# First expert's weights and early rows: a generator that runs beside the attention is started eight steps sooner and spread out

## The chip, the cores and the metric

One core of one Trainium2 chip. The metric is the device time of one launch in microseconds (us): 1130.11 us is the median of three runs before the change (1129.94 to 1133.36).

## What is computed

A decaying-attention layer on 8 x 8 heads of 576 positions, then two mixture-of-experts layers on the 4608 resulting rows of 512 numbers. In the first, each row goes to the expert with the largest logit; in the second, experts take rows greedily, 576 each.

```python
ret = scores * Dmat[None, :, :, :]              # scores = q k^T / 8, Dmat[i, j] = gamma^(i-j) for i >= j
x = np.matmul(ret, v)                           # to rows of 512: 4608 x 512
expert_idx = np.argmax(x @ w_gate, axis=1)      # first layer
for e in range(8):
    xe = x[expert_idx == e]
    out[expert_idx == e] = gate_w * (np.maximum(xe @ w1[e], 0) @ w2[e])
# second layer: the same two matmuls, with rows assigned in order of their logits, at most 576 to an expert
```

## The kernel before

**Attention** (`attention`) handles 36 tiles of 128 rows (t = 0 to 35), software-pipelined: one step `s` of the loop at its end calls each stage for another tile (loads six ahead, q and k transposed two ahead, scores one ahead, logits two behind). For a tile, PE makes the scores (24 small matmuls, L184) in the PSUM tile `pS`; DVE masks them into `sh` (L187); PE subtracts what was rounded off (L189) and DVE makes the remainder `sl` (L191); PE multiplies by the values and the running state (L214, `pO`), DVE scales the rows into `xr` (L245), PE transposes them (L152), ACT splits them (L158, L160) and PE makes eight logits (L262). There is one `pS`: the next tile's scores wait until `sl` of this one is written. Transposes, logits and the lists below share three PSUM tiles `tp`. Every three or four tiles `route` chooses experts on DVE (L273 to L288), and SP then stores the rows to `Xs`.

**Beside it runs the generator `early`**, resumed once a step from step `AFTER` on. It (1) loads the four parts of expert 0's first weight and splits each into two fp16 halves (`load_half`: ACT casts, L384; DVE or GpSimd subtracts), (2) counts which of the first 27 tiles' rows go to expert 0 and makes a list of 384 of them (matmuls L668, L669, L560; DVE rows `nA`, `G`, `lw`, `ix`, L670 to L675, L537 to L569), (3) gathers these rows with three indirect DMAs from GpSimd (L418), into the memory that later holds the second weight, and (4) normalises each group of 128: ACT squares and sums (L430), DVE makes a power of two (L311 to L313, `scA`), ACT scales (L443), DVE subtracts (L446), SP turns the result by DMA (L457). The first expert's first layer starts on these 384 columns as soon as the attention is done; its other 256 rows are gathered after that.

**What sets the order.** The kernel is written in program order, but the tile framework reorders: it runs its own time estimate (`schedule_with_timeline_sim=True`) and writes for each engine one in-order queue. Only instructions that go through `pe(...)` or `keep_in_program_order` keep their order. An instruction whose semaphore is not there yet stops its whole queue.

**After it** `moe1` runs 8 experts (`layer1` L499, `layer2` L525) and `moe2` another 8; PE is nearly always busy there.

Of the kernel before, what the change touches and what calls it, by code (L numbers as in the profile page):

```python
# [21 lines left out]
BIG = 1048576.0  # L22
TA = 27
SA = 3
AFTER = 24
T0 = (76, 88)
LATE = 3
SOON = 3
# [72 lines left out]
def attention(k, q, kk_, v, wg1, X, after):  # L101
# [197 lines left out]
    for s in range(-7, NT + 5):  # L299
        store(2 if s < NT + 2 else 36)  # L300
        for f, off in stages:
            if 0 <= s - off < NT:
                f(D[s - off])
        if s >= AFTER:
            next(after, None)
# [108 lines left out]
def gather(k, src, gidx, M=128, xg=None):  # L414
    nc = k.nc
    if xg is None:
        xg = k.fp.tile([128, W], F32, name="xg", bufs=6)
    nc.gpsimd.indirect_dma_start(out=xg[:M], out_offset=None, in_=src,  # L418
                                 in_offset=bass.IndirectOffsetOnAxis(ap=gidx[:M], axis=0))
    return xg  # L420
# [15 lines left out]
def normalise(k, xg, dve=False, to=None, pin=False):  # L436


    nc = k.nc
    h, sc = to or (k.fp.tile([128, 1024], F16, name="xhl", bufs=2), k.fp.tile([128, 6], F32, name="sc", bufs=12))  # L440
    x = xg[:, :512]
    scale2(k, x, sc, h[:, 0:512], dve, pin)
    d = nc.scalar.activation(h[:, 0:512], x, AF.Copy, scale=sc[:, 1:2])  # L443
    if pin:
        pe(k, d)
    nc.vector.scalar_tensor_tensor(h[:, 512:1024], x, sc[:, 1:2], h[:, 0:512], op0=OP.mult, op1=OP.subtract)  # L446
    nc.vector.tensor_scalar(sc[:, 3:4], sc[:, 2:3], 2.0 ** -14, None, op0=OP.mult)
    nc.gpsimd.tensor_copy(sc[:, 4:6], xg[:, 512:514])
    return h, sc


def turn(k, x, xT, s, M=128, dma=True):

    nc = k.nc
    S = slice(s * 128, s * 128 + M)
    if dma:
        nc.sync.dma_start(xT[:, :, S], x[:M], transpose=True)  # L457
        return
    pt = k.fps.tile([128, 8, 128], F16, name="tp")
    for c in range(8):  # L460
        pe(k, nc.tensor.transpose(pt[:, c, :M], x[:M, c * 128:(c + 1) * 128], k.idh[:M, :M]))
    nc.scalar.activation(xT[:, 0:4, S], pt[:, 0:4, :M], AF.Copy)
    nc.vector.tensor_copy(xT[:, 4:8, S], pt[:, 4:8, :M])


def new_xT(k):
    k.xn += 1
    return (k.xp if k.xn % 2 else k.fp).tile([128, 8, CAP1], F16, name="xT", bufs=1)
# [74 lines left out]
def lists(k, V, nt, base, end, n, slot, twice=False, begun=None, more=None):  # L543

    nc = k.nc
    G, nV = begun or cover(k, V, nt, base, end, n * 128)
    parts = [(G[:, 0], V), (G[:, 1], nV)]  # L550
    if more:
        parts += [(more[1][:, 0], more[0]), (more[1][:, 1], more[2])]
    pl = k.tp([128, 5, NS + 4])[:, :, :nt + 4]
    for s in range(n):
        cut = [(0, 128, 128 * s)]
        if twice and s == n - 1:
            cut = [(0, 64, 128 * s), (64, 128, 128 * s)]
        for lo, hi, o in cut:
            for i, (x, y) in enumerate(parts):
                pe(k, nc.tensor.matmul(pl[lo:hi, s, :], x[:, o:o + hi - lo], y, start=i == 0, stop=i == len(parts) - 1))  # L560
    N = slice(0, n)
    w = k.lp.tile([128, 5, 6], F32, name="lw")
    nc.vector.tensor_tensor(w[:, N, 0], slot[:, N], pl[:, N, nt], op=OP.subtract)
    cm = k.lp.tile([128, 5, NS], F32, name="lc")[:, :, :nt]
    nc.vector.tensor_tensor(cm[:, N], pl[:, N, 0:nt], w[:, N, 0:1].to_broadcast([128, n, nt]), op=OP.is_le)
    nc.vector.tensor_reduce(w[:, N, 1], cm[:, N], op=OP.add, axis=AX.X)
    nc.vector.scalar_tensor_tensor(w[:, N, 2], w[:, N, 1], 128.0, pl[:, N, nt + 1], op0=OP.mult, op1=OP.add)
    ix = k.lp.tile([128, 5], I32, name="ix", bufs=3)
    nc.vector.tensor_scalar(ix[:, N], w[:, N, 2], float(128 * nt - 1), None, op0=OP.min)  # L569
    return ix, pl  # L570
# [53 lines left out]
def tables(k, V, nt, incl, base):  # L624

    nc = k.nc
    nc.vector.tensor_copy(V[:, :, 0:nt], incl)
    nc.vector.tensor_copy(V[:, :, nt], base)
    nc.vector.tensor_copy(V[:, :, nt + 1], k.c('p').to_broadcast([128, V.shape[1]]))
    nc.vector.memset(V[:, :, nt + 2:nt + 4], 1.0)  # L630
# [21 lines left out]
def early(k, X, w1):  # L652


    nc = k.nc
    first = load_half(k, k.w[0], w1, 1, 2)
    next(first)
    yield
    yield
    for _ in range(4):  # L660
        next(first, None)
        yield
    k.nA = k.cp.tile([128, 4], F32, name="nA")
    OA = k.OH[:, 0, 0:TA]
    inc = k.lp.tile([128, TA], F16, name="incA", bufs=1)
    nc.vector.tensor_tensor_scan(inc, k.one_h[:, 0:TA], OA, 0.0, op0=OP.mult, op1=OP.add)
    pb = k.tp([128, 2])
    nc.tensor.matmul(pb[:, 0:1], k.lt_h, inc[:, TA - 1:TA], start=True, stop=True)  # L668
    nc.tensor.matmul(pb[:, 1:2], k.one_h, inc[:, TA - 1:TA], start=True, stop=True)  # L669
    nc.vector.tensor_copy(k.nA[:, 0:2], pb)  # L670
    nc.vector.tensor_tensor(k.nA[:, 2:3], k.nA[:, 0:1], inc[:, TA - 1:TA], op=OP.add)
    nc.vector.tensor_scalar(k.nA[:, 3:4], k.nA[:, 0:1], -1.0, 128.0 * SA, op0=OP.mult, op1=OP.add)
    V = k.lp.tile([128, 1, TA + 4], F16, name="VA", bufs=1)
    tables(k, V, TA, inc[:, None, :], k.nA[:, 0:1])
    nc.vector.scalar_tensor_tensor(OA, inc, k.nA[:, 3:4], OA, op0=OP.is_gt, op1=OP.mult)  # L675
    ix, _ = lists(k, V[:, 0, :], TA, k.nA[:, 0:1], k.nA[:, 2:3], SA, k.slot)

    g = k.wp.tile([128, 8, 512], F16, name="w2h").rearrange("p f d -> p (f d)").bitcast(F32)
    h = k.wp.tile([128, 8, 512], F16, name="w2l").rearrange("p f d -> p (f d)")
    sc = k.cp.tile([128, SA, 6], F32, name="scA")  # L680
    rows = [gather(k, X[0:128 * TA, :], ix[:, s:s + 1], xg=g[:, W * s:W * (s + 1)]) for s in range(SA)]
    k.early = new_xT(k), []
    yield
    for s in range(SA):
        yield
        x, c = normalise(k, rows[s], to=(h[:, 1024 * s:1024 * (s + 1)], sc[:, s, :]))
        turn(k, x, k.early[0], s)
        k.early[1].append(c)
# [898 lines left out]
def program(tc, q, kk, v, wg1, w11, w12, wg2, w21, w22, consts, out, dbg=None):  # L1587
    nc = tc.nc
    ctx = ExitStack()
    k = K()  # L1590
    k.pin = False
    setup(k, tc, nc, ctx, consts)
    moe_setup(k, ctx)
    X = tc.dram_tile([128 * NT, W], F32, name="Xs")
    X1 = tc.dram_tile([128 * NS, W], F32, name="X1s")
    LG = tc.dram_tile([128 * NS, 8], F32, name="LGsd")
    g1 = split_gate(k, wg1, "wg1")
    k.wgl = split_gate(k, wg2, "wg2")
    select_setup(k)
    k.w = {0: K()}  # L1600
    attention(k, q, kk, v, g1, X, early(k, X, w11[0]))
    open_ffn(k)
    rest = moe1(k, X, X1, w11, w12)
    k.pin = False
    overflow(k, X, X1, LG, w11, w12)
    k.wn, k.xn, k.yn = 8, 9, 0
    k.pin = True
    moe2(k, X1, w21, w22, out, rest)
    k.pin = False
    anew(k, X1, w21, w22, out)  # L1610
    if dbg:
        dbg(k, X, X1, LG)
    k.fctx.close()
    ctx.close()
# [25 lines left out]
```

## Time and profile before

| | |
|---|---|
| runs | 1129.94, 1130.11, 1133.36 us |
| the profiled execution | 1129.93 us, of which the span from first to last instruction is 1128.1 us |
| PE, DVE, ACT, POOL busy | 94%, 59%, 43%, 30% of the span |
| attention | about the first 221 us |
| mean granted TensorE clock | 0.978 of full |

In a row of the timeline come the start (us), the duration, engine, line and operation, output<-inputs, shapes, and in brackets how long the engine had stood idle before and what released it. A queue is in order, so a row that waits holds all behind it.

### The profile page before, as it was taken

What the parts mean: (1) busy time and instruction counts of PE and PEld (TensorE: products, weight loads), DVE (VectorE), ACT (ScalarE), POOL (GpSimd) and SP (SyncE); (2) the same over time, 40 slices, a digit from 0 to 9 for tenths busy, and PEclk for the clock granted to TensorE, in tenths of its full rate; (3) what the DMA queues carried; (4) which work ended last, traced back from release to release, by engine and by line L of the source; (5) the groups of instructions that cost most, each with busy time, mean ns of one, the idle gap of its engine ahead of it and who ended that gap; (6) DMA issues with size and microseconds to landing.
All of it is one profiled execution on the core that took longest, in us unless ns stands there. A gap on an engine that the chain in (4) does not pass through costs nothing. (4 is left out here: it accounts for less than half of the span.)

```text
span 1128.1 us, 25795 instructions
## 1 busy us (share of the span) xinstructions
PE 1061.4 (94%) x10279; PEld 682.9 (61%) x10279; DVE 668.7 (59%) x1662; ACT 481.4 (43%) x851; POOL 340.7 (30%) x589
## 2 busy tenths in 40 slices
PE   7999999789998999999989989899999999999996
PEld 5778877555646464746457534656565656567573
DVE  5787888775648455647553476747566646634140
ACT  5777766455545354536442124322233222224231
POOL 5766775041202020212040023323324141431101
PEclk9999999799999999999989999899999999999998
DMA  9999882349767677777966025538367392784211
GB/s 239 225 252 233 204 219 74 114 160 220 179 171 169 142 192 171 178 178 196 253 143 104 11 94 149 161 102 189 110 184 182 104 214 91 175 205 142 88 62 44
DMA packets 307520, 178.32 MB, mean 158 GB/s; under 512 B 241408, under 2 KB 274176, under 8 KB 307392
## 3 DMA queue, kind: packets, MB, share of 16 engines
q1 hardware_dynamic: 296928, 144.24, 52.6%
q0 software_dynamic: 10464, 32.34, 9.3%
q8 instruction: 84, 1.38, 0.5%
q14 instruction: 44, 0.36, 0.1%
HBM read 116.82 MB, written 31.28 MB: 131 GB/s over the span
## 5 line engine op out<-in xcount | busy, mean ns | idle before, releaser
L499 PE MATMUL ph<-xT,w1h 128*128 128x320 f16 (+4 forms) x2048 | 374.3, 299 | 11.9 <-DVE sc L312 4.9
L499 PEld LDWEIGHTS <-w1h 128*128 128x128 f16 x2048 | 200.3, 100 | 89.9 <-issue 24.3
L499 PE MATMUL ph<-xT,w1l 128*128 128x320 f16 (+4 forms) x1024 | 233.8, 299 | 0.0
L525 PE MATMUL py<-w2h,hh 128*128 128x512 f16 x536 | 203.2, 379 | 2.8 <-DVE key L1268 2.2
L525 PE MATMUL py<-w2l,hh 128*128 128x512 f16 x536 | 203.3, 379 | 0.0
L525 PE MATMUL py<-w2h,hl 128*128 128x512 f16 x536 | 203.2, 379 | 0.0
L525 PEld LDWEIGHTS <-hh 128*128 128x128 f16 x1072 | 103.1, 98 | 120.1 <-issue 4.9
L504 ACT ACTIVATE hh<-ph 128x576 f16<-128x576 f32 (+4 forms) x136 | 83.3, 613 | 181.7 <-PE ph L499 177.4
L505 DVE SCALAR_TENSOR_TENSOR hl<-ph,hh 128x576 f16<-128x576 f32 (+4 forms) x136 | 97.8, 719 | 69.0 <-ACT hh L504 67.9
L499 PEld LDWEIGHTS <-w1l 128*128 128x128 f16 x1024 | 100.9, 100 | 35.6 <-issue 3.3
L387 DVE SCALAR_TENSOR_TENSOR w1l<-stage,w1h 128x1024 f16<-128x1024 f32 x62 | 75.6, 1222 | 59.2 <-ACT w1h L384 58.1
L525 PEld LDWEIGHTS <-hl 128*128 128x128 f16 x536 | 52.4, 98 | 60.3
L387 DVE SCALAR_TENSOR_TENSOR w2l<-stage,w2h 128x1024 f16<-128x1024 f32 x64 | 78.3, 1224 | 12.0 <-ACT w2h L384 10.9
L384 ACT ACTIVATE w2h<-stage 128x1024 f16<-128x1024 f32 x64 | 66.9, 1048 | 8.7 <-DMA stage<-in_moe_w_dram 8.5
L430 ACT ACTIVATE x1r<-py 128x512 bf16<-128x512 f32 x40 | 23.8, 596 | 108.9 <-PE py L525 64.9
L384 ACT ACTIVATE w1h<-stage 128x1024 f16<-128x1024 f32 x62 | 64.2, 1046 | 8.7 <-DMA stage<-in_moe_w_dram 8.7
L1446 POOL DMA_INDIRECT out_dram<-x1r,ti x20 | 21.0, 1051 | 127.5 <-ACT x1r L1445 105.7
L1446 POOL DMA_INDIRECT out_dram<-w2T,ti x20 | 22.4, 1122 | 122.7 <-ACT w2T L1445 104.4
L418 POOL DMA_INDIRECT xg<-X1s,ix x40 | 44.7, 1116 | 44.2 <-DVE zf L1372 24.3
L583 POOL COPY x1r<-sc 128x1 f32<-128x1 f32 x37 | 8.5, 232 | 158.8 <-DMA X1s<-x1r 93.0
L187 DVE TENSOR_TENSOR sh<-pS,ct 128x1024 f16<-128x1024 f32 x36 | 43.9, 1220 | 17.3 <-PE pS L184 17.2
L147 POOL TENSOR_TENSOR vl<-vf,vh 128x512 f16<-128x512 f32 x36 | 41.7, 1159 | 36.1 <-ACT vh L146 28.9
(370 smaller groups left out, 1780.1 us busy)
## 6 DMA issues: line engine op xcount, KB each, us to landing
stage<-in_moe_w_dram SPq DMA_DIRECT2D x128, 512.0 KB, 4.1
Xs<-xr SPq DMA_DIRECT2D x36, 257.0 KB, 4.4
X1s<-x1r SPq DMA_DIRECT2D x33, 257.0 KB, 3.2
k<-in_k_dram SPq DMA_DIRECT2D x32, 256.0 KB, 4.3
q<-in_q_dram SPq DMA_DIRECT2D x32, 256.0 KB, 4.1
v<-in_v_dram SPq DMA_DIRECT2D x32, 256.0 KB, 4.4
k<-in_k_dram SPq DMA_DIRECT2D x8, 128.0 KB, 3.5
q<-in_q_dram SPq DMA_DIRECT2D x8, 128.0 KB, 3.7
```

What stands on the lines that cost most here:

```text
L147: nc.gpsimd.tensor_tensor(d.vl, d.vf, d.vh, op=OP.subtract)
L187: nc.vector.tensor_tensor(f(d.sh), f(pS), both, op=OP.mult)
L384: d = nc.scalar.activation(at(h, i), t, AF.Copy, scale=128.0)
L387: d = nc.vector.scalar_tensor_tensor(at(l, i), t, 128.0, at(h, i), op0=OP.mult, op1=OP.subtract)
L418: nc.gpsimd.indirect_dma_start(out=xg[:M], out_offset=None, in_=src, in_offset=bass.IndirectOffsetOnAxis(ap=gidx[:M], axis=0))
L430: d = nc.scalar.activation(q.bitcast(mybir.dt.bfloat16), x, AF.Square, accum_out=sc[:, 0:1])
L499: pe(k, nc.tensor.matmul(ph[:, z, :b], x[:, c, F], xT[:, y + c, a:a + b], start=i == 0, stop=i == 11))
L504: nc.scalar.activation(oh, src, AF.Relu)
L505: nc.vector.scalar_tensor_tensor(ol, src, 0.0, oh, op0=OP.max, op1=OP.subtract)
L525: pe(k, nc.tensor.matmul(py, x[:, f, S], y[:, f, :], start=i == 0, stop=i == 23))
L583: nc.gpsimd.tensor_copy(xr[:, 513:514], sc[:, 5:6])
L1446: nc.gpsimd.indirect_dma_start(out=out2 if tail else out, out_offset=bass.IndirectOffsetOnAxis(ap=ti, axis=0), in_=y, in_offset=None)
```

## The change

`AFTER` goes from 24 to 16. In `early` each of the four casts of the weight now comes after three resumptions (it was one), and one resumption more lies between the gathers and the first square. Counted in resumptions, the weight parts, which fell on steps 26, 27, 28 and 29, now fall on steps 19, 22, 25 and 28; the list and the gathers go from step 30 to 31, the three groups of rows from steps 32 to 34 to steps 34 to 36.

```diff
-AFTER = 24
+AFTER = 16
...
     first = load_half(k, k.w[0], w1, 1, 2)
     next(first)
-    yield
-    yield
     for _ in range(4):
+        yield
+        yield
+        yield
         next(first, None)
-        yield
+    yield
+    yield
+    yield
     k.nA = k.cp.tile([128, 4], F32, name="nA")
...
     k.early = new_xT(k), []
+    yield
     yield
     for s in range(SA):
         yield
```

What the queues show: on SP, and for all loads and casts of the first weight on ACT, DVE and GpSimd, the order is the same before and now. What moves is the list, the gathers and the normalising of the early rows. Lines from 658 on are numbered 3 to 4 higher in the changed file.

**DVE, tiles 32 to 34.** Before, ten rows from the mask of tile 32 (the first L187; `ix` of the list stands nine rows ahead of it):

```order
L187 TENSOR_TENSOR sh<-pS,ct 128x1024
L286 TENSOR_SCALAR es<-es 128x3
L245 TENSOR_TENSOR xr<-pO,ct 128x2x4x64
L288 RECIPROCAL gt<-es 128x3
L311 TENSOR_SCALAR scA<-scA 128x1
L312 TENSOR_SCALAR scA<-scA 128x1
L313 TENSOR_SCALAR scA<-scA 128x1
L191 TENSOR_TENSOR sl<-pS,ct 128x1024
L447 TENSOR_SCALAR scA<-scA 128x1
L311 TENSOR_SCALAR scA<-scA 128x1
```

Now, from the remainder of tile 32 (the first L191) on:

```order
L191 TENSOR_TENSOR sl<-pS,ct 128x1024
L566 TENSOR_REDUCE lw<-lc 128x3
L172 SCALAR_TENSOR_TENSOR kT<-tp,kT 128x512
L567 SCALAR_TENSOR_TENSOR lw<-lw,tp 128x3
L569 TENSOR_SCALAR ix<-lw 128x3
L187 TENSOR_TENSOR sh<-pS,ct 128x1024
L245 TENSOR_TENSOR xr<-pO,ct 128x2x4x64
L311 TENSOR_SCALAR scA<-scA 128x1
L191 TENSOR_TENSOR sl<-pS,ct 128x1024
L312 TENSOR_SCALAR scA<-scA 128x1
```

The list (`lw`, `ix`) is now finished one tile later, ahead of the mask of tile 33 rather than 32, and only that mask and one `xr` stand between it and the first row (L311) that needs a gathered row; route's rows, which stood between them, now come ahead of the list's end.

**GpSimd, the same place.** Before:

```order
L418 DMA w2h<-Xs,ix 128x514 x3
L448 COPY scA<-w2h 128x2
L147 TENSOR_TENSOR vl<-vf,vh 128x512
L448 COPY scA<-w2h 128x2
L290 COPY xr<-gt 128x3
```

Now:

```order
L147 TENSOR_TENSOR vl<-vf,vh 128x512
L236 TENSOR_TENSOR stl_5399<-st_5397,sth_5398 128x256
L290 COPY xr<-gt 128x3
L418 DMA w2h<-Xs,ix 128x514 x3
L236 TENSOR_TENSOR stl_5523<-st_5521,sth_5522 128x256
L448 COPY scA<-w2h 128x2 x3
```

The last `vl` and the copy of `gt` that releases the store of tiles 27 to 29 are now ahead of the gathers.

**DVE, expert 0's first layer**, the two late row groups (`xhl`) and the second part of the second weight (`w2l`). Before:

```order
L505 SCALAR_TENSOR_TENSOR hl<-ph,hh 128x384
L447 TENSOR_SCALAR sc<-sc 128x1
L446 SCALAR_TENSOR_TENSOR xhl<-xg,sc,xhl 128x512
L839 TENSOR_TENSOR sc<-sc 128x1
L387 SCALAR_TENSOR_TENSOR w2l<-stage,w2h 128x1024
L446 SCALAR_TENSOR_TENSOR xhl<-xg,sc,xhl 128x512
```

Now:

```order
L505 SCALAR_TENSOR_TENSOR hl<-ph,hh 128x384
L313 TENSOR_SCALAR sc<-sc 128x1
L843 TENSOR_TENSOR sc<-sc 128x1
L447 TENSOR_SCALAR sc<-sc 128x1
L843 TENSOR_TENSOR sc<-sc 128x1
L387 SCALAR_TENSOR_TENSOR w2l<-stage,w2h 128x1024
L446 SCALAR_TENSOR_TENSOR xhl<-xg,sc,xhl 128x512 x2
```

The weight's row now comes ahead of both `xhl` rows, and `hl` two short rows sooner. On ACT that part's cast (L384) moves ahead of both scalings (L443) in the same way. PE's queue is unchanged from the first L499 on.

## Rows read from the trace of the kernel before

**Rows 1.** The page: PE's busy time, share and instructions.
```profile
PE 1061.4 (94%) x10279; PEld 682.9 (61%) x10279; DVE 668.7 (59%) x1662; ACT 481.4 (43%) x851; POOL 340.7 (30%) x589
```

**Rows 2.** Timeline of DVE from tile 31 to tile 35.
```profile
185.86 0.16 DVE L670 COPY nA<-tp 128x2 f32<-128x2 f32 x1
...
187.20 1.23 DVE L187 TENSOR_TENSOR sh<-pS,ct 128x1024 f16<-128x1024 f32 x1
...
191.09 0.16 DVE L569 TENSOR_SCALAR ix<-lw 128x3 int32<-128x3 f32 x1
191.15 0.68 DVE L172 SCALAR_TENSOR_TENSOR kT<-tp,kT 128x512 f16<-128x512 f32 x1
...
192.90 1.21 DVE L187 TENSOR_TENSOR sh<-pS,ct 128x1024 f16<-128x1024 f32 x1
...
195.95 0.15 DVE L311 TENSOR_SCALAR scA<-scA 128x1 int32<-128x1 int32 x1 [1.09 <-ACT w2l L430]
...
196.39 1.22 DVE L191 TENSOR_TENSOR sl<-pS,ct 128x1024 f16<-128x1024 f32 x1
...
198.67 0.75 DVE L446 SCALAR_TENSOR_TENSOR w2l<-w2h,scA,w2l 128x512 f16<-128x512 f32 x1
...
200.41 1.22 DVE L187 TENSOR_TENSOR sh<-pS,ct 128x1024 f16<-128x1024 f32 x1
...
204.29 1.23 DVE L191 TENSOR_TENSOR sl<-pS,ct 128x1024 f16<-128x1024 f32 x1 [0.15 <-PE pS L189]
...
208.10 1.23 DVE L187 TENSOR_TENSOR sh<-pS,ct 128x1024 f16<-128x1024 f32 x1 [1.64 <-PE pS L184]
...
210.08 1.22 DVE L191 TENSOR_TENSOR sl<-pS,ct 128x1024 f16<-128x1024 f32 x1
...
213.00 1.21 DVE L187 TENSOR_TENSOR sh<-pS,ct 128x1024 f16<-128x1024 f32 x1
```

**Rows 3.** Timeline of POOL, first and third gather.
```profile
191.54 1.21 POOL L418 DMA_INDIRECT w2h<-Xs,ix  x1 [1.03 <-DVE ix L569]
...
194.32 0.95 POOL L418 DMA_INDIRECT w2h<-Xs,ix  x1 [0.30 <-issue]
```

**Rows 4.** Timeline of ACT, squares of the first and third gathered group.
```profile
195.19 0.63 ACT L430 ACTIVATE w2l<-w2h 128x512 bf16<-128x512 f32 x1 [1.21 <-DMA w2h<-Xs,ix]
...
199.59 0.63 ACT L430 ACTIVATE w2l<-w2h 128x512 bf16<-128x512 f32 x1 [1.08 <-DMA w2h<-Xs,ix]
```

**Rows 5.** Timeline of PE: two stalls in this stretch, and the first layer's start.
```profile
196.75 0.38 PE L159 MATMUL tp<-qTh,less 128*128 128x512 f16 x1 [0.98 <-ACT qTh L158]
...
200.84 0.58 PE L159 MATMUL tp<-xTh,less 128*128 128x512 f16 x1 [1.45 <-ACT xTh L158]
...
221.57 0.80 PE L499 MATMUL ph<-xT,w1h 128*128 128x384 f16 x2 [0.27 <-ACT lgs L264]
```

**Rows 6.** Windows: us; busy PE, PEld, DVE, ACT, POOL; granted clock; DMA share; GB/s.
```profile
200.00:210.00 10.00, 9.11 (x133) 6.25 (x132) 7.43 (x15) 6.52 (x15) 1.36 (x2) 0.66 0.45 97
...
764.00:766.00 2.00, 2.00 (x20) 1.36 (x19) 0.98 (x5) 0.00 (x0) 0.00 (x0) 0.50 0.78 255
929.00:931.00 2.00, 2.00 (x18) 1.43 (x17) 0.52 (x3) 1.12 (x2) 0.35 (x1) 1.00 0.89 307
```

**Rows 7.** Timeline of PE: two single stalls elsewhere, just ahead of the last two windows.
```profile
763.16 0.16 PE L1345 MATMUL tp<-V,lt_h 128*128 128x1 f16 x1 [2.28 <-DVE V L1334]
...
928.71 0.17 PE L1287 MATMUL tp<-r,sel 128*16 128x8 f16 x1 [2.11 <-DVE r L1283]
```

**Rows 8.** Timeline of DVE in expert 0's first layer.
```profile
235.19 0.55 DVE L505 SCALAR_TENSOR_TENSOR hl<-ph,hh 128x384 f16<-128x384 f32 x1
...
235.72 0.74 DVE L446 SCALAR_TENSOR_TENSOR xhl<-xg,sc,xhl 128x512 f16<-128x512 f32 x1
...
236.45 1.22 DVE L387 SCALAR_TENSOR_TENSOR w2l<-stage,w2h 128x1024 f16<-128x1024 f32 x1
```

**Rows 9.** Timeline of PE at the same place: the first late group is turned.
```profile
236.44 0.61 PE L461 MATMUL tp<-idh,xhl 128*128 128x128 f16 x8
```

More of the change, by code (lines that the diff above doesn't have):

```diff
@@ L657, in early @@
     next(first)
+    for _ in range(4):
+        yield
+        yield
+        yield
+        next(first, None)
     yield
     yield
-    for _ in range(4):
-        next(first, None)
-        yield
+    yield
     k.nA = k.cp.tile([128, 4], F32, name="nA")
```

## The prediction

> **What bounds the kernel now.** I read the page first: PE is busy 94% of the span [rows 1], so a change counts where PE stands still. Next I compared the queues. The weight's loads and casts stand where they stood, so the part that the change is named for moves nothing: I cost it at 0 on every engine, and its DMAs too. What moves lies in the last five tiles of the attention and in one place of expert 0's first layer, so only these two stretches were read.
>
> In the first stretch the timeline of DVE gives the tiles' pace. From mask to mask (`sh`, L187) it shows 5.7 us from tile 31 to 32, then 7.5 and 7.7, then 4.9 [rows 2]. The two long ones are the early rows' doing. The first square on ACT stands 1.21 us for the gathered rows and the third 1.08 us [rows 4]; DVE's L311 behind the first stands 1.09 us [rows 2], with the remainder of tile 32 queued behind it; and PE stands 0.98 and 1.45 us for ACT's splits, queued behind the squares [rows 5]. After that the granted clock of the stretch 200 to 210 is 0.66 [rows 6], a mixture of 2.4 and 1.2 GHz, so PE's own rows got longer. Layer 1 begins at 221.57 [rows 5], and what these tiles lose or gain moves it.
>
> **The change part by part: the tiles.** I step DVE's new queue through with the starts and durations of rows 2, since DVE's mask and remainder rows set the pace. A row's duration overlaps the next row's by nearly 0.1 (`ix`, 0.16 long, starts at 191.09, the next row at 191.15). So a mask or remainder (1.21 to 1.23) takes 1.14 us of the queue, an `xr` or kT row (0.68) 0.6, L446 (0.75) 0.66, a short row about 0.1 when it is interleaved with others.
>
> - *Mask of tile 32.* Gone from ahead of it: the list rows, about 1.0 us. Added ahead of it: the rows from `nA` to `G`, 1.34 us (185.86 to 187.20), which used to run while PE was making tile 31's scores. Interleaved with route's rows they cost a little less. Start 192.8, before 192.9.
> - *Remainder of tile 32.* Mask 1.14, `xr` 0.6, list and route rows 0.55: 195.1, where it was 196.39, as the wait of 1.09 is not in front of it now.
> - *Mask of tile 33.* Remainder 1.14, kT 0.6, three list rows 0.4: `ix` ends at about 197.3. PE's next transposes need the PSUM tile `tp` that the list gives back with L567, at 197.2, and the scores of tile 33 stand behind them in PE's queue (transposes and 24 matmuls, some 1.3 us). Start 198.6, before 200.41.
> - *The new wait.* Before, `ix` ended at 191.25, the first gather began 0.29 later at 191.54 [rows 2, 3] and its rows were there 3.65 us after that, at 195.19 [rows 4]; L311 followed 0.76 later. From 197.3 that gives 202.0 for the new L311. DVE is through with the mask and `xr` of tile 33 at 200.35, so it stands 1.65 us, longer than the 1.09 of before: one mask and one `xr` cover a gather less well than route, mask and `xr` did. Queued behind L311 is the remainder of tile 33, and behind that PE's scores of tile 34. Remainder at 202.1, before 204.29.
> - *Tile 34.* Mask at 204.8: 1.14, kT 0.6, nine short rows 0.95; before 208.10. Between this mask and its remainder now stand two L446, `xr` and three short rows (mask 1.14 and 2.1 more): 208.0, before 210.08.
> - *Mask of tile 35.* Remainder 1.14, the third L446 0.66, eight short rows 0.7: 210.5, before 213.00.
>
> So with PE at 2.4 GHz throughout the change gives **-2.5 us**. That is what it would give without the fall of the clock before, too: the same rows stepped in the old order at the full clock put the mask of tile 34 about 5.8 us behind that of tile 33, not 7.7. So the question is whether the clock falls again.
>
> *The clock.* PE now stands in one piece from its last split of tile 34's q, about 195.2, until L567 at 197.2: 2.0 us, then some 0.5 us before the mask of tile 33, and 0.7 us for the remainder of tile 33. The trace has two single stalls of about that length: after 2.28 us the two next us but one run at 0.50, after 2.11 us they run at 1.00 [rows 6, 7]. With the further stalls close behind I take it that the clock falls, and for the price that of before, 1.9 us between the two masks and a little after, **+2.0**; the bounds are 0 and 3.4. The upper one: a mean of 0.66 over 10 us is 6.8 us at the half rate, and half of them would be lost if PE set the pace in every one.
>
> *The gather's time.* 3.65 us is the first group's; the third took 5.27 us from its start (194.32 to 199.59) [rows 3, 4], beside stores of `Xs`. The store of tiles 27 to 29 now goes out ahead of the gathers, at about 195.5, and should be almost through; I take 3.65 and keep 5.27 as the upper bound, +1.6. By the Trainium skill (DMA: Bandwidth & Descriptors, Anatomy of one DMA) a GpSimd DMA takes about 2.0 us plus its bytes at 436 GB/s, by which I estimate 2.6 us for 263 kB; L311 would then wait 0.6 us and the sum be 1.05 us lower. The row of this trace disagrees, 3.65 us, and I go by the row.
>
> *The gathers' copies, the turns.* GpSimd's L448 rows now hold nothing but a 0.2 us copy, since `vl` is ahead of them; 0. SP's three turns come with the L446 rows, up to about 210; the stores behind them in SP's queue wait for a later `gt` anyway, and layer 1 reads the turned rows 9 us later; 0 as long as that cover is there.
>
> **The change part by part: expert 0's first layer.** PE turns the first late group (L461) at 236.44, just as its L446 is done [rows 8, 9]. Now the weight's L387 (1.22 us, 1.14 of the queue) stands ahead of that L446, together with a short row more; `hl` is two short rows sooner, 0.2. PE's queue has L461 four matmuls after `hl`, so PE reaches it and stands: about **+1.35 us**. ACT has cast that part already, in a wait of its own, so L387 need not wait. The second turn and all later rows follow PE, and I see nothing that takes the delay up: the later stalls of PE wait for gathers whose lists PE itself makes. Bounds 0 (were the first L446 waiting for ACT longer than I think) and 1.4.
>
> **Sum.** -2.5 + 2.0 + 1.35 = +0.85 us on the profiled execution's 1129.93, 1130.8; the median of the runs is 0.2 above that execution, so 1131.0 for the median.
>
> **The rivals.** (0.3% of this kernel, 3.4 us, is about what a measurement can tell from no change.)
>
> *A, the clock holds.* For it: a stall of 2.11 us did not bring it down [rows 7]. Against it: the other one did, and here more follow. Then -2.5 + 1.35: 1128.8 on the execution, 1129.0.
>
> *B, faster: the gather is early and the late turn is hidden.* If the first group came 2.6 us after its start, the clock held and L461 lost nothing, the sum is -2.5 - 1.05: 1126.6. Against it: both waits on ACT that the trace has for these gathers are longer [rows 4].
>
> *C, slower: the gathers meet the store.* One mechanism, at L311 of tile 33: the store of tiles 27 to 29 goes out some 2 us ahead of the gathers and shares the transfer engines with them; if the first group takes 5.27 us like the third before, DVE stands 3.3 us, PE with it, and the clock stays low over both last tiles. -2.5 + 1.6 + 3.4 + 1.35 = +3.85: 1134.0. It decides from a landing of about 5 us on. For it: the third gather. Against: that store was then just beginning.
>
> *D, the change doesn't do what it says.* True of the weight, as above, and in the sum; it leaves the times as they are.
>
> **How the numbers follow.** The forecast (the clock falls again) has 0.47, A 0.27, B 0.12, C 0.14. The forecast and A lie within 0.3%, so same 0.74, faster 0.12 (B), slower 0.14 (C). The range leaves out B's end and keeps C's: from 1127.6 (-2.5 with the late turn hidden) to 1134.0 (C).
>
> **What would show it.** In the changed profile: SP's and the casts' rows in their places; L311 of the first group idle 1.5 us or more behind ACT's square, between `xr` and the remainder of tile 33; a PE stall of about 2 us released by L567; masks of tiles 33, 34 and 35 at about 198.6, 204.8 and 210.5, later by what the clock takes; layer 1 about 0.5 us sooner than 221.57; L461 standing 1.3 us or more for L446. Wrong would be: no wait at L311 (then the gather is shorter than I think), layer 1 more than 3 us sooner or later, or no stall at L461.

## The result, and the profile after

The change made the kernel **slower**: 1138.06 us (median of five runs, 1136.45 to 1143.39) against 1130.11 (five runs, 1127.82 to 1133.36). The ratio is 1.0074, with a 95% interval of 1.0047 to 1.0101: under 1%, but clear of no change. The forecast was 1131.0 with 1134.0 as its upper end. The profiled execution took 1143.39 us, 13.5 more than that of before (1129.93), and is the slowest of the five, so its losses are above the usual.

The two stretches that the prediction read, in the profile after. The page's row of PE:

```profile
PE 1059.3 (93%) x10279; PEld 679.6 (60%) x10279; DVE 667.4 (58%) x1662; ACT 480.5 (42%) x851; POOL 338.4 (30%) x589
```

The timelines of DVE (`ix` and the masks of tiles 33 to 35) and of PE (the start of layer 1, and L461):

```profile
197.94 0.17 DVE L569 TENSOR_SCALAR ix<-lw 128x3 int32<-128x3 f32 x1
198.27 1.22 DVE L187 TENSOR_TENSOR sh<-pS,ct 128x1024 f16<-128x1024 f32 x1 [0.16 <-PE pS L184]
...
206.85 1.22 DVE L187 TENSOR_TENSOR sh<-pS,ct 128x1024 f16<-128x1024 f32 x1
...
212.73 1.21 DVE L187 TENSOR_TENSOR sh<-pS,ct 128x1024 f16<-128x1024 f32 x1
...
221.58 0.48 PE L499 MATMUL ph<-xT,w1h 128*128 128x384 f16 x2 [0.27 <-ACT lgs L264]
...
237.84 0.40 PE L461 MATMUL tp<-idh,xhl 128*128 128x128 f16 x4 [1.28 <-DVE xhl L446]
```

The window (columns as in [rows 6]):

```profile
200.00:210.00 10.00, 6.73 (x112) 4.70 (x111) 6.54 (x19) 6.75 (x17) 3.04 (x7) 1.00 0.37 89
```

Against [rows 2, 5, 6, 9]: the mask of tile 33 comes where it was forecast (198.27), that of tile 34 two microseconds later than forecast, layer 1 starts at 221.58 as before (221.57), the clock is 1.00 where it was 0.66, and PE stands 1.28 us at L461, as forecast. When PE begins the second MoE, this profile is 0.7 us ahead of before (696.63 against 697.30).

The time was lost where the prediction had not looked, in **the second MoE**. Each of its experts (a *phase* here) runs its two layers on PE while DVE chooses the rows of the next (`choose`, with a matmul that waits for `r`), GpSimd gathers them (five L418), SP turns them (L457, a transposing DMA, a *turn* below) and loads the next parts of weights (L365). I take the time between PE's first L499 of an expert and its first L525: in phase 1 (the second expert) this is 30.53 us before (757.45 to 787.98) and 37.41 after, **+6.9**; in phase 2 27.06 (814.47 to 841.53) and 32.12, **+5.1**. Phase 0, from its first L499 to that of phase 1, is 2.9 us longer too (63.1 against 60.15). Of these three only the loss of phase 1 can be put down to the change: the other two stand in a second profile of before too (e18 below: 1.4 and 5.8 us). PE's long waits there, after:

```profile
792.20 0.85 PE L499 MATMUL ph<-xT,w1h 128*128 128x288 f16 x4 [5.01 <-DVE hl L505]
...
830.49 0.17 PE L1291 MATMUL tp<-r,sel 128*16 128x8 f16 x1 [3.38 <-DVE r L1287]
```

and the longest of each kind in the same two stretches of before:

```profile
771.54 0.65 PE L499 MATMUL ph<-xT,w1h 128*128 128x288 f16 x4 [0.41 <-DVE hl L505]
...
830.85 0.17 PE L1287 MATMUL tp<-r,sel 128*16 128x8 f16 x1 [0.81 <-DVE r L1283]
```

(The two waits for `r` are not at the same place: 6.9 us into the phase after, 16.4 us before.)

In phase 1 DVE is not the cause but is held: its cast of the last weight part waits for ACT's, and that for the load. After (timelines of SP, ACT, DVE; an SP row covers several issues):

```profile
777.24 0.34 SPq L365 DMA_DIRECT2D stage<-in_moe_w_dram  x1
777.67 9.68 SPq L457 DMA_TRANSPOSE xT<-xg  x2
...
789.16 1.06 ACT L384 ACTIVATE w2h<-stage 128x1024 f16<-128x1024 f32 x1 [7.76 <-DMA stage<-in_moe_w_dram]
...
790.25 1.23 DVE L387 SCALAR_TENSOR_TENSOR w2l<-stage,w2h 128x1024 f16<-128x1024 f32 x1 [5.50 <-ACT w2h L384]
791.40 0.75 DVE L505 SCALAR_TENSOR_TENSOR hl<-ph,hh 128x576 f16<-128x576 f32 x1
```

and before:

```profile
773.70 0.38 SPq L365 DMA_DIRECT2D stage<-in_moe_w_dram  x1
776.46 6.71 SPq L457 DMA_TRANSPOSE xT<-xg  x2
...
781.56 1.06 ACT L384 ACTIVATE w2h<-stage 128x1024 f16<-128x1024 f32 x1 [2.70 <-DMA stage<-in_moe_w_dram]
...
782.65 1.23 DVE L387 SCALAR_TENSOR_TENSOR w2l<-stage,w2h 128x1024 f16<-128x1024 f32 x1 [0.44 <-ACT w2h L384]
783.79 0.75 DVE L505 SCALAR_TENSOR_TENSOR hl<-ph,hh 128x576 f16<-128x576 f32 x1
```

The load takes 11.9 us from issue to ACT's start (777.24 to 789.16), before 7.9; counted from the phase's start it lands at +29.4 instead of +24.1. The `hl` row (L505, the low halves of layer 1's result) queued behind on DVE is what PE waits for.

The change does touch this place. Ahead of the prediction I had named only the list, the gathers, the normalising and expert 0's rows as moved; that was incomplete. The framework orders each queue by its own time estimate, and the list one resumption later (e2 leaves it where it was) gives another order there too. In phase 1, DVE:

```
 ch<-P3,key
+hl<-ph,hh 128x576
 key<-key,dead
 cmp<-key,fth
 w2l<-stage,w2h 128x1024
-hl<-ph,hh 128x576
```

In phase 0 three `hl` rows shift by one to five places among the rows of `choose`. The queues of SP, POOL, ACT and PE are unchanged in the second MoE.

### The profile page after: what moved, and what is told of

It is laid out like the page before. It is cut to its first block, busy times and chain, and to the rows that moved or that the text cites. A ratio compares the mean times of both kernels' runs of the same rounds, so it can differ in the third digit from the quotient of the medians.

```text
span 1141.6 us, 25793 instructions
## 1 busy us (share of the span) xinstructions
PE 1059.3 (93%) x10279; PEld 679.6 (60%) x10279; DVE 667.4 (58%) x1662; ACT 480.5 (42%) x851; POOL 338.4 (30%) x589
## 5 line engine op out<-in xcount | busy, mean ns | idle before, releaser
L499 PE MATMUL ph<-xT,w1h 128*128 128x320 f16 (+4 forms) x2048 | 373.3, 299 | 20.4 <-DVE hl L505 8.8
L499 PEld LDWEIGHTS <-w1h 128*128 128x128 f16 x2048 | 199.7, 100 | 97.0 <-issue 32.3
L499 PE MATMUL ph<-xT,w1l 128*128 128x320 f16 (+4 forms) x1024 | 233.6, 299 | 0.0
L525 PE MATMUL py<-w2h,hh 128*128 128x512 f16 x536 | 203.6, 380 | 2.8 <-DVE key L1272 2.2
L525 PE MATMUL py<-w2l,hh 128*128 128x512 f16 x536 | 203.5, 380 | 0.0
L525 PE MATMUL py<-w2h,hl 128*128 128x512 f16 x536 | 203.5, 380 | 0.0
L525 PEld LDWEIGHTS <-hh 128*128 128x128 f16 x1072 | 103.3, 98 | 120.2 <-issue 5.0
L505 DVE SCALAR_TENSOR_TENSOR hl<-ph,hh 128x576 f16<-128x576 f32 (+4 forms) x136 | 97.6, 718 | 71.2 <-ACT hh L504 69.3
L499 PEld LDWEIGHTS <-w1l 128*128 128x128 f16 x1024 | 100.6, 100 | 38.0 <-issue 5.9
L387 DVE SCALAR_TENSOR_TENSOR w1l<-stage,w1h 128x1024 f16<-128x1024 f32 x62 | 75.6, 1222 | 59.4 <-ACT w1h L384 54.5
L525 PEld LDWEIGHTS <-hl 128*128 128x128 f16 x536 | 52.4, 98 | 60.7 <-issue 0.7
L387 DVE SCALAR_TENSOR_TENSOR w2l<-stage,w2h 128x1024 f16<-128x1024 f32 x64 | 78.3, 1223 | 14.7 <-ACT w2h L384 13.4
L384 ACT ACTIVATE w2h<-stage 128x1024 f16<-128x1024 f32 x64 | 67.0, 1048 | 11.3 <-DMA stage<-in_moe_w_dram 11.2
L384 ACT ACTIVATE w1h<-stage 128x1024 f16<-128x1024 f32 x62 | 64.2, 1047 | 8.7 <-DMA stage<-in_moe_w_dram 8.7
L418 POOL DMA_INDIRECT xg<-X1s,ix x40 | 42.7, 1068 | 43.7 <-DVE zf L1376 24.0
L187 DVE TENSOR_TENSOR sh<-pS,ct 128x1024 f16<-128x1024 f32 x36 | 43.9, 1220 | 16.5 <-PE pS L184 16.5
```

The lines of the kernel that those rows point to most:

```text
L187: nc.vector.tensor_tensor(f(d.sh), f(pS), both, op=OP.mult)
L384: d = nc.scalar.activation(at(h, i), t, AF.Copy, scale=128.0)
L387: d = nc.vector.scalar_tensor_tensor(at(l, i), t, 128.0, at(h, i), op0=OP.mult, op1=OP.subtract)
L499: pe(k, nc.tensor.matmul(ph[:, z, :b], x[:, c, F], xT[:, y + c, a:a + b], start=i == 0, stop=i == 11))
L505: nc.vector.scalar_tensor_tensor(ol, src, 0.0, oh, op0=OP.max, op1=OP.subtract)
L525: pe(k, nc.tensor.matmul(py, x[:, f, S], y[:, f, :], start=i == 0, stop=i == 23))
```

## The experiments

Each ran on a chip together with the kernel before, whose medians there were 1122.7 to 1124.2 us (a chip with a single run of before gave 1132.87). Ratios are to before on the same chip; phases are compared with the first profile of before. Where rows had to be held in place, a helper adds an order without a wait between named rows of one queue; the edits below show only such lines, and of them those that move a row. Further lines of the same kind hold the remaining rows, and SP's loads and turns, in the order of the kernel that is edited (in e3 and e12, of before).

```python
def queue(k, *rows):
    info = mybir.DependencyInfo(mybir.DependencyClass.NoSync, mybir.DependencyReason.DATA)
    for a, b in zip(rows, rows[1:]):
        k.tc.add_manual_dep(k.row[b].ins, k.row[a].ins.name, info, reason="queue")
```

**e1, the change again.** No edit.

> The changed kernel once more, unedited, for a second profile and a fresh ratio. The first profile lost 13 us in the second mixture of experts alone, in three places (PE waits 1.80, 5.01 and 3.38 us for hl, hl and r). If the loss belongs to the program, the ratio is again 1.005 to 1.010 and the same places stand still; if it was the chance of one comparison, the ratio is below 1.003.

1.0047 (1.0023 to 1.0071), just under what was expected. Phase 1 lost 4.4 us and phase 2 4.2; phase 0 lost nothing (59.98 us).

**e2, only the weight spread, the list on its old step.** The edit is the change without its last two resumptions:

```diff
     first = load_half(k, k.w[0], w1, 1, 2)
...
     yield
     yield
-    yield
     k.nA = k.cp.tile([128, 4], F32, name="nA")
...
     k.early = new_xT(k), []
-    yield
     yield
```

> Only the weight's part of the change: the casts on resumptions 19, 22, 25 and 28, while the list stays on 30 and the groups of rows on 32 to 34. Every engine's queue is then that of before, row by row. All theories: ratio 1.000, within 0.002. Anything else would mean that something besides the queues' order has changed.

The queues that result are, row by row, those of the one before: spreading the weight moves nothing. It was still measured at 1.0033 (1.0011 to 1.0055). So the same program can come out 0.3% off, and outside its interval: a ratio of 1.002 to 1.004 alone shows nothing here.

**e3, the change's attention with all later rows in before's order.** On top of the change:

```diff
+    queue(k, ("xl", 3), ("w2l", 1), ("xl", 4))
...
+    queue(k, ("hl", 88), ("L567", 12))
+    queue(k, ("hl", 89), ("ch", 2))
+    queue(k, ("cmp2", 0), ("hl", 90), ("s1s2", 0), ("hl", 91))
+    queue(k, ("w2l", 36), ("hl", 97))
```

> The changed kernel with every row after the attention pinned to the order of before (expert 0's first layer on DVE and ACT, phases 0 and 1 of the second mixture of experts on DVE); only the attention's queues are the changed ones. Theory 1 (the moved DVE rows of the second mixture of experts make the loss): 1.000, within 0.002. Theory 2 (their order is nothing; the attention's new times shift when gathers, turns and weight loads meet later): 1.005 to 1.010, with PE waits of several us for hl in phase 1.

1.0005 (0.9981 to 1.0029); phase 1 +0.04, phase 2 +0.8. On the same chip the mean of e1's 12 runs is 5.1 us above that of e3's (95%: 2.4 to 7.8). So most of what the change loses lies in the rows behind the attention.

**e4, the reverse: before, with the second MoE's DVE rows as the change has them.**

```diff
+    queue(k, ("P3", 1), ("hl", 88), ("ftodo", 1))
+    queue(k, ("ch", 2), ("hl", 89), ("key", 2))
+    queue(k, ("hl", 91), ("s1s2", 0))
+    queue(k, ("ch", 3), ("hl", 97), ("key", 3))
```

> The kernel before with only the DVE rows of phases 0 and 1 of the second mixture of experts moved as in the changed kernel: hl behind the list and ahead of the search's first rows; attention and expert 0 as before, SP's queue as before. Theory 1 (the moved rows make the loss): 1.005 to 1.010, with PE waits for hl in phase 1 of 3 us or more. Theory 2: 1.000, within 0.002.

1.0019 (0.9996 to 1.0043): the time does not show the loss that was expected, and PE's wait for `hl` was 1.41 us, not 3. In its profile, the slowest of its 12 runs, phase 1 lost 1.6 us and phase 2 6.0, without any change in the attention.

**e5 and e16, only the last of these lines** (phase 1), **e6 and e15, only the first three** (phase 0).

> The kernel before, with only one VectorE row of the second MoE moved as the change moves it: in layer 1 of that MoE's second expert the low-half split hl (L505) stands ahead of the key's add and the compare instead of behind the weight cast L387. Theory 1, this move lets the third gather be issued some 0.5 us earlier, so that the gathers and the transposing loads collide and the fourth weight load lands late: phase 1 (757 to 788 us of before) loses 1.5 to 7 us with a PE wait for hl of 1.2 to 5 us (0.5 in before), phase 2 (814 to 841) loses 4 to 6 us with a PE wait for r of 3 to 4.3 us (0.8 in before). Theory 2, the moved rows of phase 0 set it: both phases stay within 1 us of before. Theory 3, the collision comes by chance in any kernel: then it may be seen here, but also in e6 and not tied to the rows.

> The kernel of e5 again (only the phase 1 row moved), one look. Theory 1: phase 1 loses 1.5 to 7 us with a wait of PE for hl over 1 us; phase 2 within 1 us if the phase 0 rows set that one. If e5 was chance, phase 1 is within 0.5 us.

> The kernel before, with only the other moved VectorE rows of the second MoE, those of its phase 0 (hl of rows block 0 behind five router rows, of block 1 behind the choice, of block 3 ahead of the sum). Theory 1 (the phase 1 row does it): phases 1 and 2 within 1 us of before, time within 0.3% of before. Theory 2 (these rows do it): phase 1 loses 1.5 to 7 us and phase 2 4 to 6 us, with PE waits for hl of over 1.2 us and for r of over 3 us.

> The kernel of e6 again (only the phase 0 rows moved), one look. If these rows set the loss of phase 2: 2 to 6 us lost there with a wait of PE for r of 3 us or more, phase 1 within 0.5 us. If it was chance in e6: phase 2 within 1 us.

e5 1.0035 (1.0012 to 1.0059), e6 0.9996 (0.9972 to 1.0021). Phase 1: +2.0 and +0.8 with the phase 1 row (the second under the 1.5 expected), +0.3 and +0.9 without (the second over the 0.5 expected). Phase 2: +0.2 and +0.1 with the phase 1 row, +2.2 and +5.2 with the phase 0 rows. By their times neither can be told from e2, which changes nothing. Against theory 1 the two losses have different companions.

**e9 and e17, the change with the phase 1 row alone put back.**

```diff
+    queue(k, ("P3", 1), ("hl", 88), ("ftodo", 1))
+    queue(k, ("ch", 2), ("hl", 89), ("key", 2))
+    queue(k, ("hl", 91), ("s1s2", 0))
+    queue(k, ("w2l", 36), ("hl", 97))
```

> The change with one VectorE row put back: in phase 1 of the second MoE the split hl stands behind the compare and the weight cast L387 again, as before; all other rows as the change has them. If that row alone makes the loss of phase 1, its PE wait for hl is at most 0.6 us and the phase stands within 0.5 us of before (the change lost 6.9 and 4.4 us in its two profiles). Phase 2 may still lose 2 to 6 us, since e6 lost 2.2 us there with hl in its old place. The time then lies between the change and before, 1 to 3 us under the change. If the loss of phase 1 comes by chance or from the rows of phase 0, it is there again with 1.5 us or more.

> The kernel of e9 again (the change with the phase 1 row put back), one look. Phase 1 within 0.5 us of before (theory 1). If the phase 0 rows set the loss of phase 2, 2 to 6 us there; if e9's 0.1 us was the rule for this kernel, within 1 us.

e9: 1.0024 (1.0005 to 1.0044). Phase 1 -0.02 and -0.45: the loss is gone. Phase 2 +0.1 in e9, a miss for the phase 0 rows.

**e10 and e18, the kernel before against itself.**

> The kernel before itself, measured against itself: what the comparison gives for no change at all. Theory 3 (chance): its profile may show a loss in phase 1 or 2 too. If the rows decide, phase 1 stands within 0.5 us of the first profile. The ratio shows how far from 1 an unchanged kernel can come out; e2, an identical program, came out at 1.0033.

> The kernel before again, one look. Phases 1 and 2 within 1 us of its first profile if the moved rows are what makes the loss; 2 us or more in either if it can come with before's order too.

e10: 1.0015 (0.9990 to 1.0040); phase 1 +0.7, phase 2 -0.3. e18's phase 1 lost 1.0. Both losses of phase 1, with before's order, are outside what was expected.

In phase 2 e17 lost 4.9 us and e18, which is before, 5.8. The profile after shows the same thing, here DVE in after and in e18:

```profile
829.74 0.44 DVE L1285 TENSOR_TENSOR s1s<-tp,ct 128x64 f16<-128x64 f32 x1 [6.66 <-remote]
```

```profile
819.62 0.44 DVE L1281 TENSOR_TENSOR s1s<-tp,ct 128x64 f16<-128x64 f32 x1 [6.46 <-remote]
```

In all three DVE and ACT stand until about 6 us into the phase and start again within 0.1 us of each other; in the other 17 profiles the same rows start at 0.5 and 0.25 us. In these three alone phase 0 is long too (63.1, 61.5 and 61.5 us, elsewhere 58.8 to 60.2), and 8 to 9% of the records of DMA landings are missing, against at most 0.4%. What holds the engines there is not known, but it comes with before's order as well. So these three tell nothing of phase 2, and the +2.9 and +5.1 of the profile after are not shown to be the change's.

**e12, the load late.** Before, with the load one turn later on SP:

```diff
+    queue(k, ("turn", 77), ("load", 87), ("turn", 78))
```

> The kernel before with one edit on SP: in phase 1 of the second MoE the fourth weight load is issued behind the third transposing load instead of behind the second. All VectorE rows as before. If the late landing of this load is what holds the phase up, the load is issued near +20 us of the phase instead of +16.3, lands after +27 and PE waits 1 us or more for hl, with phase 1 longer by 1 to 6 us. If something else that comes with the moved hl row holds it up, phase 1 stays within 0.5 us of before.

A miss. The load was issued at +20.0 but landed at +24.45, and phase 1 lost 0.35. How late the load is issued does not decide alone; it took 4.4 us from there, in before 7.8.

**e7 and e14, the change with the weight loads ahead of the turns; e8 and e11, before with the same.**

```diff
+    queue(k, ("load", 87), ("turn", 75), ("turn", 76), ("turn", 77), ("turn", 78), ("load", 88), ("turn", 79))
+    queue(k, ("load", 93), ("load", 94), ("turn", 80), ("turn", 81), ("turn", 82), ("turn", 83), ("turn", 84), ("load", 95))
```

> The change, with the weight loads that follow the gathers issued ahead of the transposing loads on SP in phases 1 and 2 of the second MoE (one load and two loads), all else in the change's order. If the loss is the late landing of those loads behind the transposing loads, the waits of PE for hl in phase 1 (5.0 us in the change's profile) and for r in phase 2 (3.4 us) fall to under 1 us each, both phases stand within 1.5 us of before, and the time is that of before or up to 5 us below. If the waits were for something else (the gathered rows themselves), the transposing loads come later still and the phases stay 4 us or more above before.

> The change, unedited, a third time. Phase 1 of the second MoE loses 2 to 7 us against the first profile of before (its hl row is moved: theory 1), phase 2 4 to 5 us if the phase 0 rows set it. Ratio 1.004 to 1.007.

> The kernel of e7 again (the change with the weight loads ahead of the transposing loads in the two phases), beside e13 on one chip. If the two phases hold the change's loss, its ratio is 0.003 to 0.006 under that of e13 and its phases 1 and 2 stand within 1 us of before. If the loss lies elsewhere, the two ratios are within 0.002.

> The kernel before, with the same loads issued first. If the loads are late in before too now and then, its time falls by 1 to 4 us and its waits for hl and r in phases 1 and 2 stay under 1 us; if they are hidden in before, it stays within 0.3%, or loses 0.5 to 2 us through the later transposing loads.

> The kernel of e8 again, with more rounds: if the loads issued first really save about 2 us, the ratio is 0.997 to 0.999 again with its upper bound under 1; if e8 was a lucky draw, it is within 0.0015 of 1.

One store on GpSimd (`out_dram<-w2T`) moves by two places in phase 2 as well.

e7 1.0003 (0.9981 to 1.0024). e13 (the change) and e14 on one chip: 1.0053 (1.0026 to 1.0081) and 1.0016 (0.9991 to 1.0040); the means of their 12 runs, 1130.4 and 1125.8 us, differ by 4.6 us (95%: 1.7 to 7.4). e13 lost 4.5 and 4.3 us in the two phases, e14 0.1 and -0.95. (The profiles show more than the times: e13's is the slowest of its 12 runs, e1's the second slowest.) ACT's wait for the load, in e13:

```profile
784.81 1.06 ACT L384 ACTIVATE w2h<-stage 128x1024 f16<-128x1024 f32 x1 [5.65 <-DMA stage<-in_moe_w_dram]
```

and e14's SP and ACT, where no wait is left:

```profile
767.46 0.37 SPq L365 DMA_DIRECT2D stage<-in_moe_w_dram  x1
767.95 8.29 SPq L459 DMA_TRANSPOSE xT<-xg  x4
...
774.60 1.05 ACT L384 ACTIVATE w2h<-stage 128x1024 f16<-128x1024 f32 x1
```

On the kernel before the same order gave 0.9983 (0.9965 to 1.0001) and 0.9993 (0.9974 to 1.0012): perhaps 0.1%, not shown; by what was expected of e11, e8 was a lucky draw. No version beats both kernels by what can be measured.

**All profiles together.** Time over the first profile of before in each phase (us), and when the load of phase 1 lands, from the phase's start. In brackets stand the losses of phase 2 in the three profiles set aside above:

| kernel | phase 1 row | load lands | phase 1 | phase 0 rows | phase 2 |
|---|---|---|---|---|---|
| e2, e3, e9, e17 | old | 21.5, 21.8, 22.1, 23.0 | -0.03, 0.04, -0.02, -0.45 | old, old, moved, moved | 0.2, 0.8, 0.1, (4.9) |
| before, e6, e12 | old | 24.1, 24.1, 24.5 | 0, 0.3, 0.35 | old, moved, old | 0, 2.2, 0.45 |
| e10, e15, e18 | old | 24.8, 25.0, 25.1 | 0.7, 0.9, 1.0 | old, moved, old | -0.3, 5.2, (5.8) |
| e16, e4, e5 | moved | 24.9, 25.7, 26.1 | 0.8, 1.6, 2.0 | old, moved, old | 0.05, 6.0, 0.2 |
| e1, e13, after | moved | 26.9, 27.2, 29.4 | 4.4, 4.5, 6.9 | moved | 4.2, 4.3, (5.1) |
| e7, e14 (loads first) | moved | 18.5, 19.0 | 0.03, 0.1 | moved | -0.95, -0.95 |
| e8, e11 (loads first) | old | 17.9, 19.2 | -0.3, 0.2 | old | -0.95, -0.95 |

Phase 1's loss follows the landing almost line by line: none up to 24.5, then more with every microsecond. In the change that landing is set by one DVE row: moved 26.9 to 29.4 (three profiles), put back 22.1 and 23.0 (two).

Between e5 (+2.0) and e1 (+4.4) the loss jumps, though the landing is only 0.8 us later. Most of that is the clock. Windows of 3.2 us (columns as in [rows 6]) just behind PE's wait for `hl`, in e5 and in e1:

```profile
780.10:783.30 3.20, 3.20 (x26) 2.22 (x26) 1.31 (x6) 0.00 (x0) 0.00 (x0) 1.00 0.97 316
```

```profile
786.40:789.60 3.20, 3.20 (x15) 1.76 (x15) 1.28 (x5) 0.00 (x0) 0.00 (x0) 0.50 1.01 326
```

In e16, e4 and e5 PE stood 1.27 to 1.70 us for `hl`, and the granted clock stayed at 1.00. In e1, e13 and after it stood 2.65, 2.90 and 5.01 us, and then the clock was 0.50 (1.2 GHz) for some 3.4 us: about 1.5 us of their losses.

How a row on DVE reaches a DMA shows on POOL. Before:

```profile
769.87 1.78 POOL L418 DMA_INDIRECT xg<-X1s,ix  x1 [0.30 <-issue]
771.95 0.95 POOL L418 DMA_INDIRECT xg<-X1s,ix  x1 [0.30 <-issue]
773.20 1.66 POOL L418 DMA_INDIRECT xg<-X1s,ix  x1 [0.31 <-issue]
...
769.61 1.22 DVE L387 SCALAR_TENSOR_TENSOR w2l<-stage,w2h 128x1024 f16<-128x1024 f32 x1
...
772.83 1.22 DVE L387 SCALAR_TENSOR_TENSOR w2l<-stage,w2h 128x1024 f16<-128x1024 f32 x1
```

After:

```profile
772.58 1.13 POOL L418 DMA_INDIRECT xg<-X1s,ix  x1 [0.30 <-issue]
774.01 0.95 POOL L418 DMA_INDIRECT xg<-X1s,ix  x1 [0.30 <-issue]
775.26 0.95 POOL L418 DMA_INDIRECT xg<-X1s,ix  x1 [0.30 <-issue]
...
772.80 1.22 DVE L387 SCALAR_TENSOR_TENSOR w2l<-stage,w2h 128x1024 f16<-128x1024 f32 x1
...
776.65 1.22 DVE L387 SCALAR_TENSOR_TENSOR w2l<-stage,w2h 128x1024 f16<-128x1024 f32 x1
```

A gather that begins inside an L387 takes longer to issue, here 0.7 us. Before, the third begins 0.26 us into one; with `hl` ahead, L387 begins 0.22 us after the gather, which takes 1.13. In all profiles it is 1.78 with the old row, and 1.12 to 1.31 with the moved one. The fourth gather then follows the third after 1.43 to 1.62 us instead of 2.08, the second turn, issued beside them, takes 1.85 to 2.08 us to issue instead of 1.25, and the load behind it goes out 0.5 to 1.25 us later than the 16.3 of before (before's order itself gives 15.9 to 16.7). That this spacing is what makes the transfers slow is argued from these rows and was not tried alone; e12 speaks against the lateness of the load as such.

**Open.** In phase 2, PE waits for `r`, in e13:

```profile
838.45 0.17 PE L1291 MATMUL tp<-r,sel 128*16 128x8 f16 x1 [3.76 <-DVE r L1287]
```

Without the three profiles set aside and with SP's order kept, phase 2 lost 2.2 to 6.0 us in 5 of the 6 with the phase 0 rows moved, and at most 0.8 in the 7 without. In those five the fifth gather lands 8.1 to 9.4 us after its start (4.8 to 6.4 in the other eight), the fourth turn takes 3.6 to 4.7 us to issue (1.8 to 2.6), and the load behind it goes out at +10.9 to +11.5 (+7.9 to +10.0). In after, e17 and e18 that gather takes 4.4 to 5.7 us: a second sign that their loss is another one. How much is lost hangs on the clock too: e6 waited 3.03 us for `r` and ran on at 1.00, e15, the same program, waited 3.66 and then had 0.50 for some 6.8 us. But the programs do not differ in phase 2: in e15, which lost 5.2, and e16, which lost nothing, the gathers there are issued within 0.02 us of the same offsets and only the landings differ (the fifth gather 8.5 us against 4.8). What the rows have to do with that is not known. Nor is it known why the load of phase 1 lands 0.8 us and more later in the three full kernels than in e4, e5 and e16.

## Why the prediction was wrong

**The step that failed** is in its first paragraph: "What moves lies in the last five tiles of the attention and in one place of expert 0's first layer, so only these two stretches were read." Four more DVE rows move in the second MoE, in a stretch with PE waits for DVE; they had no term, and the forecast no rival with them. In phases 1 and 2 the change lost 8.5 and 8.8 us in the profiles e1 and e13, and in the profile after 6.9 us in phase 1; by the times of e13 and e14 it is 4.6 us (1.7 to 7.4). That the moved rows bring it is shown for phase 1 (put back, the loss is gone); for phase 2 it is only a companion.

By its own steps:

- *The weight at 0*: right; e2 is the program before, row by row.
- *The tiles, -2.5*: wrong in its largest row. `ix` and the mask of tile 33 came within 0.8 us of the forecast in the profile after, but DVE's L311 then stood 3.36 us (e1) and 3.92 us (e13), not 1.65, for the gathered rows; in the profile after DVE was held for PE at that place, so I read the other two. From the first gather's start to its square were 4.5 and 5.1 us, where 3.65 was taken. That is **rival C's wait**, near its price of 3.3 us. The 2.6 us that I estimated from the Trainium skill (DMA: Bandwidth & Descriptors, Anatomy of one DMA) for such a gather are further off still. The premise that failed is that the store of tiles 27 to 29 would be almost through: in e1 its three parts were issued from 196.3 to 198.3 and landed up to 201.7, beside the gather that began at 198.43. That the store makes the gather slow agrees with this, but was not tried alone.
- *The clock, +2.0*: the fall is not fixed by the kernel. The 22 us from 200 on had a mean of 0.82 in the first profile of before and 0.87, 0.90 and 1.00 in three of the change; in 200 to 218 it was 1.00 in 7 of the 12 profiles with before's attention and in 4 of the 8 with the change's. The stall of 2.28 us of [rows 7], with 0.50 behind it, had 1.00 behind it in e18, the same program: a single stall in one trace was no ground to choose between the forecast and rival A. The first profile of before, on which the sum was made, has the latest start of layer 1 of the 12 profiles with before's attention (218.9 to 221.6, mean 220.1). The eight with the change's have 221.4 to 222.6, mean 221.7: the tiles and the clock are **+1.7 us**, not -0.5. e3's and e14's mean times, 1.4 and 1.7 us above before, agree, though within what an unchanged kernel shows.
- *The late turn, +1.35*: the stall was there, 1.28 us in all three profiles of the change. But the layer's length is 39.2 us (mean of the seven profiles with these rows moved) against 38.7 (the other thirteen; both scatter by 1.0 to 1.2 us): a loss nearer 0.4 than 1.35, as far as this tells. So something takes most of the delay up, contrary to "I see nothing that takes the delay up"; what it is was not tried.

Sum: some 1.7 us from the attention and 4.6 (1.7 to 7.4) from the second MoE, of which 0.95 is what the loads' order gains on before and so no loss of the change: together 5.3 us, where e13's mean stands 6.3 above before's. The rest is within the interval.

That layer 1 starts in the profile after where it did before (221.58 and 221.57), close to the forecast, is luck: the later tiles and the clock that did not fall cancel there.

## What to carry to other kernels

Where a framework orders the queues, compare the whole program's order and give every moved row a term or a reason, also those a long way from the edit; a row that hardly costs anything by itself can change the spacing of transfers. Look at the landings of loads that share the DMA engines with gathers and turns, and issue first what the compute waits for first, as e14 did. See whether a profile's loss stands in a second profile of the kernel before as well, before it is put down to the change. And a price taken from one profile of before is a sample: the first one here was 1.5 us off the mean in the very stretch that was argued about.

## What was not expected of the hardware

- The same program, measured against itself, gave 1.0015 and 1.0033, the second with an interval that leaves out 1.
- A GpSimd gather that begins during a 1.22 us DVE cast takes 1.66 or 1.78 us to issue, instead of 0.95 or 1.13. In all 20 profiles, 141 gathers of the second MoE begin with 0.2 to 1.2 us of such a cast left, and every one of them ends 0.81 to 0.89 us after the cast. The Trainium skill (SBUF — State Buffer, SBUF: two separate sides) has a rule of this kind: a DVE operation with two inputs in SBUF and a GpSimd operation that reads SBUF share a pair of ports, and whichever begins first keeps the other out. The rows agree: the cast that began first keeps its 1.22 us, and the gather behind it loses 0.65 us of the 0.96 that the cast had still to run.
- After PE had stood 2.65, 2.90 and 5.01 us for `hl` in phase 1, the clock was 0.50 for some 3.4 us each time; after the 2.28 us for `V` in the same phase it was 0.50 in before and 1.00 in e18, which is the same program.
- One and the same weight load took between 4.2 us (e7, issued ahead of the turns) and 11.9 us (after), and a gather of phase 1 between 3.5 us (the first ones) and 10.5 us (the fifth, before, among turns).
